# All of the second product in seven products, with casting loads and TensorE turns

## The chip, the cores and the metric

The kernel runs on one core of one Trainium2 chip. The metric is device time in microseconds (us), the median of several runs. One more execution was taken with the hardware profiler; durations in this text come from that one.

## The reference

Two stages. The first is linear attention with decay, for 4 batches, 8 heads, 768 positions and 64 features per head, computed in blocks of 64 positions with a running state; the second is a two-layer network with SiLU over the 3072 positions.

```python
for b in range(nb):                                  # 12 blocks of 64
    intra = np.einsum('bhic,bhjc->bhij', qb, kb) * Dmask[None]
    intra = np.einsum('bhij,bhjd->bhid', intra, vb)
    inter = np.einsum('bhid,bhde->bhie', qb * lam_pow[None], kv_state)
    out[:, :, sl] = intra + inter
    kb_dec = kb * rev_pow[None]
    kv_state = lam_block[None, :, None, None] * kv_state + np.einsum('bhsd,bhse->bhde', kb_dec, vb)
...
h = x @ w_in                       # 3072 x 512 by 512 x 2048
g = h * (1.0 / (1.0 + np.exp(-h)))
return (g @ w_out).astype(np.float32)   # 3072 x 2048 by 2048 x 512
```

All inputs and the output are 32-bit floats; the kernel's matmuls take bf16 and accumulate in 32 bits.

## The kernel before

**Units, sets, groups.** A unit is 128 positions of one batch, named (n, b): six values of n ("blocks 0 to 5" in the change's title) by four batches, 24 units. `rank` orders them: (0,0), (1,0), (0,1), (1,1) and so on for the first eight, then by n and batch. A set is two units whose k, q and v are loaded and prepared together: sets 0 to 3 pair n = 0 and 1 of a batch, sets 4 and 5 are n = 2, 6 and 7 are n = 3, 8 and 9 are n = 4, 10 and 11 are n = 5. A group is what the first product works on: four groups of two units (256 tokens), then four groups of four units (512 tokens).

**Loads.** SP's queue loads k, q and v of each set in 32 bits (`load_set`, lines 349 and 351), 0.5 MB each, into the buffers `ra` and `rb`. POOL's queue loads w_in and w_out in four slices each, cast to bf16 on the way (lines 364 and 367); a small `gate` copy (line 331) on POOL holds a slice back until k of a certain set has landed.

**Attention.** `prepare` casts k and q to bf16 (`kq`, on DVE or ACT), scales v (`vd`, on DVE or POOL) and turns k and q (`kqT`). Sets 0 to 3 are turned by TensorE (line 442: 8 transposes per burst, then two copies out of PSUM), sets 4 to 11 by a DMA transpose on SP's queue (line 622). Scores (`st_ps`), states (`d_ps`) and outputs (`x_ps`) are short bursts on TensorE (lines 463 to 543 and 647 to 687); masks, state updates (`yf`, `y`, `xf`, `xe`) and the evacuation to `xt` follow on DVE, ACT and POOL.

**First product.** `product1` (line 830) multiplies w_in by xt into a PSUM bank, and ACT writes SiLU of it to g (line 839). The last group goes through `product1_spared` (line 944): a two-by-two division of both factors with seven products in place of eight (Winograd's form), four rounds `jp`, with sums S1 to S4 of w_in and T1 to T4 of xt made by DVE. A round's seven products alternate between two PSUM banks P and R. After the first, P is copied to SBUF (`keep`), and further products accumulate on P; the products on R are completed by adding a kept copy (`total_of`, DVE).

**Second product.** The first eight units go through `product2_plain` (line 861): 16 matmuls of 512 columns per unit, one bank, one evacuation to `osb`, one store. The other 16 units go through `product2` and `products_of` (line 1072) in quads of four units, in the same seven-product form: sums `s` and, in place, `g` of the features (twelve on DVE, four on POOL per quad), sums `wsum` of w_out (`sums_of_w_out`; T1 overwrites a quarter of w_out, so it waits for all plain units), seven products of 16 matmuls of 256 columns, three copies of P (`keep`), three results that add a kept copy to R, and one plain copy of P. The last quad is divided into two parts that alternate.

**Order.** Nothing of this order is written by hand. Every piece is a `Task` with a priority key, the engines that it may run on with a cost for each, its dependencies and its buffers. `Planner.order` simulates the engines and three DMA queues and gives out tasks one by one; a task goes to the engine on which the plan ends it first. The program is then issued in that order; each engine works strictly in its order. Buffers come from small pools (`rb` 6, `kq` 3, `g` 18, `s` 12, `bank` 8 and others), and tasks that hold a counting buffer (`one`, `two`, `att`) limit how many banks each stage may hold.

Of the kernel before, what the change touches and what calls it, by code (L numbers as in the profile page):

```python
# [37 lines left out]
class Planner:  # L38

    LAT = {"PE": 0.23, "ACT": 0.06, "DVE": 0.06, "POOL": 0.08, "SP": 0.0}  # L40
    BEGIN = {"PE": 0.8, "ACT": 8.3, "DVE": 4.5, "POOL": 4.7, "SP": 0.8}
    FIRST, LAST, AHEAD = {"SP": 1.9, "ACT": 1.15, "POOL": 2.5}, 1.0, 0.75
# [13 lines left out]
    def order(self):  # L56
# [63 lines left out]
        while len(out) < len(self.tasks):  # L120
# [9 lines left out]
            for e in free:  # L130
# [8 lines left out]
                while ready[e]:  # L139
# [12 lines left out]
                    mine = now + t.on[e]  # L152
                    if any(max(free[o], now) + d < mine - 1e-9 for o, d in t.on.items() if o != e):
                        kept.append((key, i, t))
                        continue
# [33 lines left out]
def kernel(  # L189
# [27 lines left out]
    FRESH, TURNED, ALONE, LEAD = 4, 4, 6, 6.5  # L217
    SEQUENCE = "s0 i0 s1 i1 i2 s2 i3 o0 s3 o1 o2 o3 s4"
    POOLS = dict(bank=8, ra=3, rb=6, kq=3, kqT=3, vd=3, st=3, xe=6, xf=3, y=2, yf=2,
                 xt2=2, xt4=2, g=18, s=12, m=3, osb=3, one=3, two=4, att=6)  # L220
    BY_POOL, IN_BY_POOL, PLAIN, SPARED = (4,), (), 8, 1
# [116 lines left out]
    def load_set(key, si):  # L338
        n, b = sets[si][0]
        nb = 2  # L340
        rs = [Buf("ra" if si in (0, 3) else "rb") for _ in range(3)]
# [4 lines left out]
        def go(e, i):  # L346
            if n < PAIRED:
                tile_of(rs[i], [128, H, 2, 64], F32, "raw")
                nc.sync.dma_start(out=rs[i].tile.rearrange("p h e d -> p h (e d)"), in_=x[i])
            else:  # L350
                nc.sync.dma_start(out=tile_of(rs[i], [128, 2 * H, 64], F32, "raw"), in_=x[i])

        for i in range(3):
            ts.append([add((key, i), {"SP": 0.55}, lambda e, i=i: go(e, i), bufs=[rs[i]], nbytes=0.524,
# [55 lines left out]
    def key_of(si):  # L410
        u = rank[sets[si][0]]
        return u - 4.0 if sets[si][0][0] == 0 else u - LEAD
# [145 lines left out]
    def prepare(si):  # L558
# [7 lines left out]
        o.kq, o.kqT, o.vd, o.st = Buf("kq"), Buf("kqT"), Buf("vd"), Buf("st")  # L566
# [6 lines left out]
        def kq_of():  # L573
            return tile_of(o.kq, [128, nb, 2, NP, 2, 64], BF16, "kq")

        def kqT_of():
            return tile_of(o.kqT, [128, nb, 2, NP, U], BF16, "kqT")
# [9 lines left out]
        def cast(e, j, i):  # L587
            src = rs[i].tile[:, j * H:j * H + H, :].rearrange("p (m h) d -> p m h d", h=2)
            dst = kq_of()[:, j, i]
            copy(e, dst, src)  # L590

        ck = [[add((s - 1.0, i), {"DVE": 0.43, "ACT": 0.63}, lambda e, j=j, i=i: cast(e, j, i), deps=(lk, lq)[i],
                   bufs=[rs[i], o.kq]) for i in range(2)] for j in range(nb)]
        after("k", [t for ts in ck for t in ts])
# [10 lines left out]
        if si < TURNED:  # L605
            for j in range(nb):
                bank = Bank(fills=False)

                def turn(e, j=j, bank=bank):
                    t = tile_of(bank, [128, 2, NP, U], BF16, "tr")  # L610
                    for i in range(2):
                        for m in range(NP):
                            nc.tensor.transpose(t[:, i, m, :], kq_of()[:, j, i, m], ident)

                tr = add((s - 0.7, j), {"PE": 0.46}, turn, deps=ck[j], bufs=[bank, o.kq])
                for i in range(2):
                    o.turned.append(add((s - 1.0, 2), {"DVE": 0.43, "ACT": 0.6},
                                        lambda e, j=j, i=i, bank=bank: copy(e, kqT_of()[:, j, i], bank.tile[:, i]),
                                        deps=[tr], bufs=[bank, o.kqT]))
        else:  # L620
            def dma_turn(e):
                nc.sync.dma_start_transpose(kqT_of().rearrange("p b i m s -> p (b i m) s"),
                                            kq_of().rearrange("p b i m h d -> p (b i m h d)"))
# [4 lines left out]
    def first_part(o):  # L628
# [12 lines left out]
        def states(e):  # L641
            for j in range(nb):
                for m in range(NP):
                    for c in halves_of_d:
                        r = halves[c]
                        for p, rp in enumerate(halves):
                            nc.tensor.matmul(d_of(c)[rp, j, m, :], lhsT=o.kq_of()[r, j, 0, m, p, :],  # L647
# [3 lines left out]
        def scores(e):  # L651
            for j in range(nb):
                for m in range(NP):
                    for p, rp in enumerate(halves):
                        t = tile_of(st_ps[p], [128, nb, NP, 64], F32, "st_ps")
                        for c, r in enumerate(halves):
                            nc.tensor.matmul(t[r, j, m, :], lhsT=o.kqT_of()[rp, j, 0, m, r], rhs=o.kqT_of()[rp, j, 1, m, r],  # L657
# [6 lines left out]
    def second_part(o):  # L664
# [18 lines left out]
        def inter(e):  # L683
            for c in range(2):
                for j in range(nb):
                    for m in range(NP):
                        nc.tensor.matmul(x_of(c)[:, j, m, :], lhsT=o.xe[c].tile[:, (bs[0] + j) % 2, m, :],  # L687
                                         rhs=o.kqT_of()[:, j, 1, m, halves[c]],
# [196 lines left out]
    def sums_of_w_in():  # L885
# [6 lines left out]
        every = [t for o in infos for ts in o.ck for t in ts]  # L892

        def total(name, a, b, op, deps, on):
            done[name] = [add((on, 8), {"POOL": 2.4} if name in IN_BY_POOL else {"DVE": 0.70}, lambda e, ks=ks: tt(
# [3 lines left out]
        on = rank[groups[-SPARED][0]] - 4.0  # L899
# [6 lines left out]
    def product1_spared(gi, wbufs, wdone):  # L906
# [13 lines left out]
        done = {b: xt_done[gi] + xt_done[-1] for b in ("B11", "B21", "B22")}  # L920

        def total(name, a, b, op, deps, bufs):
            done[name] = [add((u0 - 2.0, 7), {"DVE": 0.42}, lambda e: tt(e, X(name), X(a), X(b), op), deps=deps, bufs=[x] + bufs)]
# [5 lines left out]
        for jp in range(4):  # L929
            P, R = Buf("bank"), Buf("bank")  # L930
            held = [P, R, Buf("att"), Buf("att")]
# [24 lines left out]
            wide, narrow = Buf("rb"), Buf("vd")  # L956

            def wide_of(wide=wide):
# [214 lines left out]
```

## Time and profile before

| | |
|---|---|
| median of 3 runs | 208.62 us (208.38 to 209.31) |
| the profiled execution, whole time | 207.82 us |
| its span, first to last instruction | 206.1 us |
| TensorE (PE) busy | 187.0 us, 91% |
| VectorE (DVE) busy | 134.8 us, 65% |
| ScalarE (ACT) busy | 107.4 us, 52% |
| GpSimd (POOL) busy | 52.4 us, 25% |
| mean granted TensorE clock | 0.989 |
| moved by DMA | 33.92 MB |

Shares are averages over the span; the page also cuts it into 40 slices of 5.15 us and gives each engine's busy share there in tenths. A group line names the source line, engine, operation, the tiles written and read, the shapes and the count; then busy time and the mean of one in ns; then the idle time before and who ended it. A line of the chain gives start, length and what ran. Many vector operations share line 320 (`tt`) and copies lines 313 (ACT) and 315 (DVE), so these are told apart by their tiles.

### The profile page before, as it was taken

The page shows a single profiled execution, that of the slowest core. Times are in us where ns is not written, and L with a number is a line of the kernel's source. Part 1 is how long each engine was busy: PE and PEld are TensorE (multiplying, and loading weights), DVE is VectorE, ACT ScalarE, POOL GpSimd, SP SyncE. Part 2 cuts the span into 40 slices and gives each one's busy share as a digit, 9 for nine tenths or more (in the row PEclk, how much of TensorE's full clock was granted, in tenths as well). Part 3 has the DMA queues.
Part 4 walks back from the last instruction along what each step waited for, and adds up shares of the span by engine and source line. Part 5 has one row for each costly group of instructions (what it writes and reads, how often), then busy time and mean ns, then how long its engine had stood idle before and what let it go on. Part 6 is the DMA issues. An engine that isn't in the chain of part 4 may idle for free.

```text
span 206.1 us, 5719 instructions
## 1 busy us (share of the span) xinstructions
PE 187.0 (91%) x2445; PEld 132.9 (64%) x2464; DVE 134.8 (65%) x249; ACT 107.4 (52%) x195; POOL 52.4 (25%) x76
## 2 busy tenths in 40 slices
PE   0459399999999999999999999998999999999993
PEld 0347288786667565544578648474675778888882
DVE  6488632767950467716989953999758995665411
ACT  3637267874336453375734492745615453766420
POOL 7231400401130111222565013346003221222200
PEclk9999889999999999999999999999999999999999
DMA  3999999999999999999999999905101110102213
GB/s 99 292 253 260 228 222 265 235 199 214 228 238 249 156 216 231 238 219 195 263 213 234 203 213 240 244 7 117 39 3 54 51 54 0 54 0 102 88 52 118
DMA packets 88617, 33.92 MB, mean 165 GB/s; under 512 B 67088, under 2 KB 87568, under 8 KB 88592
## 3 DMA queue, kind: packets, MB, share of 16 engines
q1 hardware_dynamic: 79232, 23.60, 57.3%
q0 software_dynamic: 4224, 4.19, 12.2%
q10 hardware_dynamic: 5136, 5.77, 8.7%
q8 instruction: 19, 0.31, 0.7%
q14 instruction: 6, 0.05, 0.1%
HBM read 27.27 MB, written 6.29 MB: 163 GB/s over the span
## 4 chain that ended last, share of the span: by engine, by line
PE 82%; DMA 8%; DVE 7%; issue 1%; ACT 0%; POOL 0%; POOLq 0%; DVEq 0%
PE h_ps L830 31%; PE o_ps L1072 22%; PE o_ps L861 13%; PE h_ps L944 6%; DMA w_in_bf<-in_moe_w_in_dram 5%; DMA raw<-in_k_dram 3%; PE x_ps L687 2%; DVE s L320 2%; PE tr L442 2%; DVE g L320 1%; PE d_ps L647 1%; PE x_ps L679 1%; PE st_ps L657 1%; PE x_ps L538 1%; DVE kq L315 1%
## 5 line engine op out<-in xcount | busy, mean ns | idle before, releaser
L830 PE MATMUL h_ps<-xt,w_in_bf 128*128 128x256 bf16 (+1 forms) x439 | 75.7, 322 | 4.7 <-DMA w_in_bf<-in_moe_w_in_dram 3.3
L839 ACT ACTIVATE g<-h_ps 128x512 bf16<-128x512 f32 x80 | 47.1, 594 | 45.7 <-PE h_ps L830 45.0
L830 PEld LDWEIGHTS <-w_in_bf 128*128 128x128 bf16 x448 | 43.7, 99 | 30.1 <-DMA w_in_bf<-in_moe_w_in_dram 3.5
L861 PE MATMUL o_ps<-w_out_bf,g 128*128 128x512 bf16 x118 | 29.7, 379 | 0.6 <-issue 0.2
L320 POOL TENSOR_TENSOR s<-g,s 128x512 bf16<-128x512 bf16 x16 | 19.0, 1188 | 43.1 <-DVE s L320 26.8
L320 DVE TENSOR_TENSOR st<-st_ps,tri 128x512 bf16<-128x512 f32 x32 | 20.5, 681 | 11.2 <-PE st_ps L657 11.2
L1072 PEld LDWEIGHTS <-g 128*128 128x128 bf16 x256 | 24.9, 98 | 4.4 <-ACT g L839 0.3
L320 DVE TENSOR_TENSOR xt<-x_ps,lam_xe 128x512 bf16<-128x512 f32 x24 | 15.9, 699 | 15.2 <-PE x_ps L687 9.5
L1072 PEld LDWEIGHTS <-s 128*128 128x128 bf16 x192 | 18.7, 98 | 2.6
L861 PEld LDWEIGHTS <-g 128*128 128x128 bf16 x128 | 12.1, 98 | 12.0
L320 POOL TENSOR_TENSOR vd<-raw,lam_v 128x512 bf16<-128x512 f32 x10 | 13.3, 1334 | 25.1 <-DMA raw<-in_v_dram 19.7
L313 ACT ACTIVATE kq<-raw 128x512 bf16<-128x512 f32 x27 | 16.2, 621 | 2.1 <-DMA raw<-in_q_dram 1.6
L320 DVE TENSOR_TENSOR osb<-o_ps,m 128x512 f32<-128x512 f32 (+1 forms) x15 | 8.7, 583 | 10.9 <-ACT m L313 6.8
L1072 PE MATMUL o_ps<-wsum,g 128*128 128x256 bf16 x128 | 15.3, 272 | 0.0
L1072 PE MATMUL o_ps<-w_out_bf,s 128*128 128x256 bf16 x128 | 15.3, 273 | 0.0
L442 PE MATMUL tr<-ident,kq 128*128 128x128 bf16 x64 | 7.0, 260 | 8.8 <-POOL gate L331 6.9
L1072 PE MATMUL o_ps<-w_out_bf,g 128*128 128x256 bf16 x128 | 15.0, 273 | 0.0
L320 DVE TENSOR_TENSOR s<-g 128x512 bf16<-128x512 bf16 x16 | 8.2, 510 | 10.4 <-ACT g L839 6.6
L313 ACT ACTIVATE m<-o_ps 128x512 f32<-128x512 f32 (+1 forms) x14 | 7.0, 503 | 11.4 <-PE o_ps L1072 11.4
L320 DVE TENSOR_TENSOR vd<-raw,lam_v 128x512 bf16<-128x512 f32 x14 | 9.2, 681 | 5.0 <-DMA raw<-in_v_dram 5.0
L313 ACT ACTIVATE osb<-o_ps 128x512 f32<-128x512 f32 (+1 forms) x12 | 6.7, 562 | 10.4 <-PE o_ps L861 6.5
L315 DVE CAST kq<-raw 128x512 bf16<-128x512 f32 x21 | 9.1, 451 | 3.8 <-DMA raw<-in_k_dram 2.0
(88 smaller groups left out, 215.1 us busy)
## 6 DMA issues: line engine op xcount, KB each, us to landing
raw<-in_k_dram SPq DMA_DIRECT2D x12, 512.0 KB, 8.2
raw<-in_q_dram SPq DMA_DIRECT2D x12, 512.0 KB, 8.5
raw<-in_v_dram SPq DMA_DIRECT2D x12, 512.0 KB, 8.0
out_dram<-osb ACTq DMA_DIRECT2D x20, 256.0 KB, 3.6
w_in_bf<-in_moe_w_in_dram POOLq DMA_DIRECT2D x4, 512.0 KB, 10.0
w_out_bf<-in_moe_w_out_dram POOLq DMA_DIRECT2D x4, 512.0 KB, 11.7
out_dram<-osb ACTq DMA_DIRECT2D x4, 128.0 KB, 1.7
out_dram<-osb SPq DMA_DIRECT2D x4, 128.0 KB, 1.7
```

Source lines behind the costliest of these rows:

```text
L313: nc.scalar.activation(o, i, AF.Copy)
L315: nc.vector.tensor_copy(o, i)
L320: (nc.vector if e == "DVE" else nc.gpsimd).tensor_tensor(o, a, b, op=op)
L442: nc.tensor.transpose(t[:, m, a], o.kq_of()[:, i, m, a], ident)
L538: nc.tensor.matmul(t[rh, m], lhsT=o.vd_of()[r, 2 * m + h, a, :], rhs=o.st_of(h)[r, m, a], start=m == 0 and a == 0, stop=True, skip_group_c ...
L647: nc.tensor.matmul(d_of(c)[rp, j, m, :], lhsT=o.kq_of()[r, j, 0, m, p, :], rhs=o.vd_of()[r, j, 2 * m + p, :], start=j == 0 and m == 0, sto ...
L687: nc.tensor.matmul(x_of(c)[:, j, m, :], lhsT=o.xe[c].tile[:, (bs[0] + j) % 2, m, :], rhs=o.kqT_of()[:, j, 1, m, halves[c]], start=False, s ...
L830: nc.tensor.matmul(t[:, j, :], lhsT=w_in_bf[:, ko, 128 * (m1 + j):128 * (m1 + j) + 128], rhs=xt[gi].tile[:, ko, :], start=(ko == 0), stop= ...
L839: nc.scalar.activation(t[:, half * per:half * per + per], bank.tile, AF.Silu)
L861: nc.tensor.matmul(t, lhsT=g.tile[:, j, 128 * gp:128 * gp + 128], rhs=w_out_bf[:, ko, :], start=(ko == 0), stop=(ko == KO - 1))
L944: nc.tensor.matmul(t[:, j, :], lhsT=W[w]()[:, k2, f:f + 128], rhs=X(r)[:, k2, :], start=first and j == 0 and k2 == 0, stop=True, skip_grou ...
L1072: nc.tensor.matmul(t[:, i_, :], lhsT=src(j)[:, k2, 128 * r:128 * r + 128], rhs=W[w]()[:, 2 * j + k2, :], start=first and i_ == 0 and j == ...
```

## The change

- `product2_plain` is used for no unit (`PLAIN` 8 to 0): the first eight units become two more quads of the seven-product form. T1 of w_out no longer waits for plain units. The first quad holds two of the four `two` buffers.
- `ONTO`: in the quads from rank 12 on, and in `product1_spared`, the first product on P is copied to the second bank R (by ACT or DVE), and the second product accumulates onto it; the result is then read from R alone. In `product1_spared` the SiLU of 1024 columns becomes two of 512, the first read straight from R.
- `CASTING`: k and q of sets 8 to 11 are loaded by DMAs on POOL's queue that cast to bf16, into one `rb` buffer laid out as `kq`; their casts go. The layout of `kq` and `kqT` of sets 4 to 11 puts k and q outermost.
- `TURNED` 4 to 6: sets 4 and 5 are turned by TensorE.
- In the planner, work on DVE is charged 0.2 us more when an engine is chosen (`BIAS`); costs of the sums are raised; the sums of w_in get a fixed priority (`SUMS_ON`) and wait for other tasks than before (`SUMS_AFTER`); the T sums of the last group no longer hold products back until the last xt.

```diff
+    BIAS = {"DVE": 0.2}
...
-                    mine = now + t.on[e]
-                    if any(max(free[o], now) + d < mine - 1e-9 for o, d in t.on.items() if o != e):
+                    mine = now + t.on[e] + self.BIAS.get(e, 0.0)
+                    if any(max(free[o], now) + d + self.BIAS.get(o, 0.0) < mine - 1e-9 for o, d in t.on.items() if o != e):
...
-    FRESH, TURNED, ALONE, LEAD = 4, 4, 6, 6.5
+    FRESH, TURNED, ALONE, LEAD = 4, 6, 6, 6.5
...
-                 xt2=2, xt4=2, g=18, s=12, m=3, osb=3, one=3, two=4, att=6)
-    BY_POOL, IN_BY_POOL, PLAIN, SPARED = (4,), (), 8, 1
+                 xt2=2, xt4=2, g=18, s=12, m=3, osb=3, one=3, two=4, att=6, sp=2)
+    BY_POOL, IN_BY_POOL, PLAIN, SPARED = (4,), (), 0, 1
+    CASTING, SUMS_AFTER, HURRY, SUMS_ON, HOLD, ONTO = 8, 16, 0.0, 9.0, 1, 12
...
+            elif si >= CASTING and i < 2:
+                tl = tile_of(rs[0], [128, 2, 2, NP, 2, 64], BF16, "kq")
+                nc.gpsimd.dma_start(out=tl[:, i].rearrange("p b m h d -> p (b m h) d"), in_=x[i])
...
+            if si >= CASTING and i < 2:
+                t = pool_task(add((key, i), {"POOL": 0.8}, lambda e, i=i: go(e, i), bufs=[rs[0]], nbytes=0.524, kind=CAST,
+                                  prior=pool_last[-1:] + raw[si - 1][1][2], late=2.0))
+                ts.append([t])
+                continue
...
-        o.kq, o.kqT, o.vd, o.st = Buf("kq"), Buf("kqT"), Buf("vd"), Buf("st")
+        o.kq, o.kqT, o.vd, o.st = rs[0] if si >= CASTING else Buf("kq"), Buf("kqT"), Buf("vd"), Buf("st")
...
-        every = [t for o in infos for ts in o.ck for t in ts]
+        every = [t for o in infos if rank[o.n, o.bs[0]] < SUMS_AFTER for t in o.cv] + [t for o in infos[:CASTING] for ts in o.ck for t in ts]
...
-        on = rank[groups[-SPARED][0]] - 4.0
+        on = SUMS_ON
...
-        done = {b: xt_done[gi] + xt_done[-1] for b in ("B11", "B21", "B22")}
+        done = {b: xt_done[gi] for b in ("B11", "B21", "B22")}
...
-            held = [P, R, Buf("att"), Buf("att")]
+            held = [P, R, Buf("sp")]
...
             m1 = product(0, P, "A11", "B11", True, [])
-            b1, c1 = keep("kqT", [m1])
-            m2 = product(1, R, "A12", "B21", True, [])
-            e11 = total_of(lambda w=wide_of: w()[:, :, lo], wide, b1, [m2, c1])
+
+            c1 = add((u0 - eager, 5), {"ACT": 0.6, "DVE": 0.69}, lambda e, P=P, R=R, f=bank_of: copy(e, f(R), f(P)), deps=[m1], bufs=[P, R])
+            m2 = product(1, R, "A12", "B21", False, [c1])
+            s11 = silu((low, lo), lambda R=R, f=bank_of: f(R), [m2], [R])
             m6 = product(2, P, "S2", "T2", False, [c1])
...
-            s1 = silu(lambda b=low: g_of(b), wide_of, 1.05, [e11, e12], [low, wide])
+            s12 = silu((low, hi), lambda h_of=h_of: h_of("12"), [e12], [narrow["12"]])
...
-        held = [P, R] + [Buf("two") for _ in range(2 * np_)]
+        held = [P, R] + [Buf("two") for _ in range(2 if u0 == PLAIN and HOLD else 2 * np_)]
...
         m1 = product(0, P, "A11", "B11", True, [])
-        b1, c1 = keep(0, [m1])
-        m2 = product(1, R, "A12", "B21", True, [])
-        e11 = result(0, lo, R, b1, [m2, c1])
+        if u0 >= ONTO:
+            c1 = add((s - eager, 5), {"ACT": 0.17 + 0.215 * np_, "DVE": 0.15 + 0.27 * np_},
+                     lambda e: copy(e, bank_of(R), bank_of(P)), deps=[m1], bufs=[P, R])
+            m2 = product(1, R, "A12", "B21", False, [c1])
+            e11 = result(0, lo, R, None, [m2])
+        else:
+            b1, c1 = keep(0, [m1])
+            m2 = product(1, R, "A12", "B21", True, [])
+            e11 = result(0, lo, R, b1, [m2, c1])
```

## The prediction

> **What bounds the kernel now.** I read the page's busy shares and slices first, then the busy time by stretches of 10 us, then the chain that ended last, then the groups by form. The page:
>
> ```profile
> PE 187.0 (91%) x2445; PEld 132.9 (64%) x2464; DVE 134.8 (65%) x249; ACT 107.4 (52%) x195; POOL 52.4 (25%) x76
> PE   0459399999999999999999999998999999999993
> DVE  6488632767950467716989953999758995665411
> DMA  3999999999999999999999999905101110102213
> ```
>
> The reader should see a PE row of nines from the eighth slice to the last but one, a DVE that is crowded only in places, and a DMA row that is full for the first 25 slices and then nearly empty. The table by stretches says how full the PE is (columns: window, its length, then PE, PEld, DVE, ACT, POOL busy, granted clock, DMA share, GB/s):
>
> ```profile
> 20.00:30.00 10.00, 6.66 (x132) 5.11 (x117) 5.43 (x11) 4.50 (x10) 2.41 (x5) 0.83 1.19 225
> 30.00:40.00 10.00, 9.95 (x148) 8.43 (x148) 4.18 (x9) 7.61 (x15) 2.41 (x4) 1.00 1.10 253
> 60.00:70.00 10.00, 9.89 (x125) 6.51 (x126) 0.87 (x2) 5.11 (x9) 1.04 (x1) 1.00 1.07 196
> 140.00:150.00 10.00, 9.32 (x58) 5.73 (x60) 8.26 (x14) 5.32 (x10) 3.15 (x3) 1.00 0.37 80
> 180.00:190.00 10.00, 10.00 (x94) 8.98 (x92) 6.20 (x12) 6.36 (x12) 2.29 (x2) 1.00 0.15 52
> ```
>
> From 30 to 200 us the PE is busy 168.2 of 170 us, at full granted clock. The only larger hole is one of 0.69 us at 140.6. So after about 24 us, when the second slice of w_in lands, time is the sum of PE work, plus 3.6 us of tail from 202.5 to 206.1. What the PE does in each piece, and its price, is in the chain (start, length, what):
>
> ```profile
> 13.71 10.23 DMA w_in_bf<-in_moe_w_in_dram
> 40.72 0.45 PE tr L442 x8
> 63.67 1.73 PE o_ps L861 x8
> 105.61 6.99 PE o_ps L1072 x64
> 140.58 0.05 issue
> 190.28 12.24 PE o_ps L1072 x112
> ```
>
> The profiled execution took 207.82 us for a span of 206.1; the median of the runs is 208.62. I work on the 207.82 and scale to the median at the end.
>
> **Products (removes PE work).** Eight 128-token units now use line 861: 16 matmuls of 512 columns each, 128 in all. The chain has 1.73 us per 8, so 27.7 us. Two quads of seven products replace them: 14 products of 16 matmuls of 256 columns, 224 in all. 6.99 us per 64 gives 24.5 us. Saving: 3.2 us, all on the PE and so on the path.
>
> **Turns of sets 4 and 5 (adds PE work).** Each set has two bursts of 8 transposes; 0.45 us per 8, four bursts, 1.8 us on the PE. Eight PSUM copies come with them (0.42 us on DVE or 0.60 on ACT, groups kqT<-tr), about 4 us, beside a DVE that has 0.87 us of work from 60 to 70 us. In return two DMA transposes leave SP's queue. Their issues hold SP 3.78 us (at 57.3) and 5.90 us (at 65.1), with the v load of set 5 queued behind the first and q, v of set 6 behind the second. Those loads move up by up to 9.7 us in all. This buys no PE time directly: it brings the first 512-token group, whose xt comes at 85 us now, nearer to 75.
>
> **Sums and evacuations (adds DVE, ACT, POOL work).** Each new quad needs 16 sums: 12 on DVE at 0.51, 0.42 and 0.61 us (rows s<-g, s<-s,g, g<-g), so 6.1 us, and 4 on POOL at 1.19, so 4.8 us. Two quads: 12.3 us of DVE, 9.5 us of POOL. They have 14 evacuations where there were 8, 6 more at 0.6 to 0.69, about 4 us. Hidden: DVE is free for 14 us between 50 and 80 (7.70, 0.87 and 7.10 busy), POOL for more. Without that cover up to 12 us would be late, and whoever reads the sums is the PE.
>
> **Casting DMAs (removes casts, moves issues).** Sixteen casts go (0.42 us on DVE, 0.62 on ACT): 6.7 to 9.9 us, off the path. Eight issues move from SP to POOL, whose queue also holds the xe blocks, the vd scalings and the fourth sums. Nearest row: the weight loads at line 364 and 367, 0.75 to 0.80 us an issue at 528 packets each. A k or q load has 2048 rows of 256 B, so between 0.75 us and four times that, 3.0 us: 6 to 24 us of POOL over some 50 us. I take 1 us each, nearest to the row; POOL is busy 25%. Each issue waits in POOL's order for a free buffer and for the previous set's v; behind it stand sums that a quad waits for. I cost it at 0, because between 100 and 160 us the PE always has a quad or a 512-token group in hand; without this cover, one late sum costs what the DVE chain at 129 to 140 us cost now, 0.69 us. Landing sooner is worth nothing either: the last loads go out at 127 and the PE has 42 us of work after the last xt at 160.6.
>
> A rule of the Trainium skill speaks against this edit. In the trace, POOL's vd at 55.87 took 2.81 us where its median is 1.04, while DVE ran wsum and kq casts beside it. The Trainium skill's page SBUF — State Buffer (Who interferes with whom) says that a DVE copy or cast in a 2-port mode locks GpSimd out, and that descriptors of a DMA issued from GpSimd are written through that port. By that rule each issue could wait behind such a cast. No row here shows a held issue.
>
> **First product copied to the second bank (moves a wait).** In the last three quads and in line 944's four rounds, the second product now waits for the copy of the first. One copy is 0.59 us (0.38 in the half-width parts). What was queued behind the first product on the PE is the second product; it can no longer follow at once. Cover: the chain alternates lines 944 and 1072 from 160 to 190, and the two halves of the last quad from 190.3 on, pieces of 0.44 to 1.75 us. I take 0; uncovered, 7 waits of 0.6 us, 4 us. In return four adds of 0.69 us leave DVE, and one SiLU of 1.05 becomes two of 0.6. DVE is not what PE waits for there (10.00 busy), so a gain of nothing. The planner's bias of 0.2 moves copies from DVE (65%) to ACT (52%); ACT takes 0.62 where DVE takes 0.42, so the startup chain, which has four kq casts and kqT copies, may lose or gain some 0.5 us. I take 0.
>
> **The early hole.** Plain units are the filler between 37 and 53 us, about 4.7 us of line 861. A quad cannot start there so freely: it needs both its groups' features, w_out's later slices (issued at 37.4 to 39.6, 11.7 us to landing), and sums made at 52.8 to 56.5. What can step in is line 830 of the third group (xt at 41.8 to 43.1): by 52.6, 160 of 192 available matmuls were done, so 32, or 3.5 us, and the first product, 1.75. But between 37.2 and 43.2 there are 1.77 us of plain work and only 0.87 us of line 830 to take its place. I charge 0.9 us, and set against it the 0.69 us hole at 140.6 and 0.2 us of small ones, since the supply comes earlier there.
>
> **Sum:** -3.2 + 1.8 + 0.9 - 0.9 = -1.4 us. 207.82 becomes 206.4; the median 208.62 becomes 207.2. About 0.5%, or 1.0 us, is what a measurement of this kernel can tell from no change.
>
> **Rivals.**
>
> *More than the sum: 205.6.* Loads that come ten us sooner, and a lighter DVE, close holes that I left open: the startup (gate copy at 13.59 behind an xe cast that waited 5.05 us for DVE, ahead of the 10.23 us weight load) up to 0.9, the middle 0.7. For it: the startup counts one to one. Against: the first loads and the gates are unedited.
>
> *Slower: quads 0 and 1 stand alone, 210.9.* Within a quad the first bank's fourth product follows its third with only a copy between: 0.6 us plus some 0.5 of hand-over. Line 830 fills such gaps in the quads of now. If nothing is there to fill them in the two new quads, the PE waits 1.1 us in each, and 0.6 more where the second quad's sums need s buffers of the first (12, all taken by one quad). The early hole stays and the holes at 140 are not closed: -1.4 + 0.9 + 2.2 + 0.6 = +2.3 us, 210.1 on the profiled run, 210.9 as a median. It decides if the PE's share from 40 to 75 us falls below nine tenths. For it: evacuations and sums take turns there with attention's own masks (DVE 8.12 from 40 to 50). Against: 11.3 us of line 830 (104 of the 256 matmuls of the first four groups) is still undone at 55 and can be mixed in, and DVE is idle from 60 to 70.
>
> *No change: POOL's queue gives it back, 208.6.* At 3.0 us an issue, eight issues add 24 us to a POOL that has 17.6 us of work from 90 to 140, and sums or xe blocks behind an issue come up to 3 us late. Two holes like the 0.69 us one at 140.6 would eat the 1.4. The rule on locked descriptors would work the same way. For it: the 2.81 row. Against: a quad's fourth sum is needed only by its last product.
>
> **Chances.** Forecast 0.50, more 0.15, slower 0.21, no change 0.14. The forecast's own range is 206.4 to 208.2, from the startup's 0.5 both ways and an uncovered wait or two; 0.43 of its 0.50 lies below 207.6, so faster by over 0.5% is 0.43 + 0.15 = 0.58. Within 0.5%: 0.07 of the forecast, 0.10 of the POOL case: 0.17. Slower: the rest, 0.25. The range that leaves out 2 in 10 goes from just under the gaining rival, 205.4, to the slow one, 210.9.
>
> **What would show it.** In the new profile line 861 is gone, line 1072 has 672 matmuls (448 now) at the same 1.75 per 16, and line 442 has 96. PE busy falls from 187.0 to about 185.6. A PE row with an eight or less between 40 and 75 us would show the slow rival; POOL issues over 2 us, with PE waits on s at 100 to 150, the POOL case. A first line 830 burst that starts other than at 24 us would show the startup moved. If PE busy itself is not 1.4 lower, the count is wrong. DMA should go slack before 125 us; if it does and the time does not move more, supply was not the bound.

## The result and the profile after

The changed kernel takes 210.09 us (median of 20 runs) beside 207.90 for the kernel before in runs on the same chips: 1.0102 times as long, 95% interval 1.0071 to 1.0132. The forecast was 207.2 against a median of 208.62, a gain of 0.7%. It came out 1.0% slower. Single executions of the kernel before spread from 206.05 to 209.31 and each profile is of one execution (for u_turn, u_onto and n_hold_s4a_on one of the longest, 224.17, 213.14 and 214.13 us), so below, ratios judge a kernel and profiles show where its time lies.

The changed kernel's profiled execution took 210.04 us with a span of 208.3. The page, its busy shares and rows:

```profile
PE 186.2 (89%) x2592; PEld 144.2 (69%) x2592; DVE 142.1 (68%) x252; ACT 111.6 (54%) x206; POOL 76.3 (37%) x100
PE   0459698989999997999997899999999999999993
DVE  6387822999999998946895983997653353555411
DMA  3999999999899999999999999800100210102203
```

PE busy fell, by 0.8 us (187.0 to 186.2). PE idle rose by 3.0 us (19.1 to 22.1), and the two together are the 2.2 us by which the span grew. DVE's row is a run of nines from the eighth slice to the fifteenth, where before it had digits down to 0. The table by stretches, same columns as before the change:

```profile
30.00:40.00 10.00, 9.27 (x144) 7.94 (x141) 5.01 (x10) 7.06 (x14) 2.68 (x5) 1.00 1.12 250
40.00:50.00 10.00, 9.21 (x198) 7.72 (x196) 9.83 (x19) 6.37 (x13) 3.25 (x6) 1.00 1.17 184
60.00:70.00 10.00, 10.00 (x199) 8.78 (x197) 10.00 (x16) 6.90 (x13) 3.91 (x5) 1.00 1.22 226
70.00:80.00 10.00, 8.21 (x170) 6.98 (x168) 9.94 (x17) 4.81 (x9) 6.19 (x7) 1.00 1.08 228
110.00:120.00 10.00, 7.79 (x158) 5.61 (x157) 7.84 (x11) 1.81 (x3) 8.76 (x9) 1.00 1.33 202
140.00:150.00 10.00, 10.00 (x161) 7.40 (x159) 7.30 (x13) 4.01 (x7) 3.10 (x3) 1.00 0.09 29
```

Two groups of holes are new: 3.8 us between 30 and 90 (0.6 before) and 2.2 us between 110 and 120 (0.2 from 90 to 120 before). After 120 us the PE has none; the hole at 140 is gone. Holes by stretch, PE idle in us, are the figure that the experiments use:

| | 30 to 90 | 90 to 120 | 120 to 150 |
|---|---|---|---|
| before | 0.6 | 0.2 | 0.85 |
| after | 3.8 | 2.2 | 0.0 |

The timeline of the PE names the longest of them; the brackets give the idle time ahead of the piece and what ended it:

```profile
42.32 2.78 PE L842 MATMUL h_ps<-xt,w_in_bf 128*128 128x256 bf16 x24 [0.79 <-DVE xt L322]
79.87 0.41 PE L699 MATMUL x_ps<-kqT,xe 128*128 128x64 bf16 x8 [1.37 <-POOL xe L319]
112.19 0.45 PE L669 MATMUL st_ps<-kqT 64*64 64x64 bf16 x32 [1.26 <-DMA kqT<-kq]
117.65 2.75 PE L842 MATMUL h_ps<-xt,w_in_bf 128*128 128x512 bf16 x12 [0.95 <-DVE xt L322]
```

and the chain that ended last shows how the third came about, a transpose that took 15.8 us from issue to landing:

```profile
94.79 1.53 PE o_ps L1086 x14
96.32 15.83 DMA kqT<-kq
...
112.38 1.05 POOL xf L322
...
113.46 1.36 DVE xe L317
```

The transposes by tile, first before, then after. Their number fell from 8 to 6, and the longest landing went from 8.7 to 15.8 us:

```profile
L622 SPq DMA_TRANSPOSE kqT<-kq x8: 1960/4807/5900, 57.3 to 140.3; - x8
DMA to landing us min/median/max: 4.5/6.8/8.7
```

```profile
L634 SPq DMA_TRANSPOSE kqT<-kq x6: 2796/4788/11888, 76.8 to 128.9; - x6
DMA to landing us min/median/max: 5.8/10.9/15.8
```

One stretch of DVE and of POOL, from the timelines of the changed kernel (its first row is DVE's, the others POOL's), shows what "full" means for DVE:

```profile
67.34 3.69 DVE L322 TENSOR_TENSOR s<-g 128x512 bf16<-128x512 bf16 x2
```

```profile
66.96 1.04 POOL L322 TENSOR_TENSOR xf<-y,lam_be 128x512 f32<-128x512 f32 x1 [0.27 <-PE h_ps L842]
68.07 0.68 POOL L319 CAST xe<-xf 64x512 bf16<-64x512 f32 x1
68.72 2.03 POOL L322 TENSOR_TENSOR vd<-raw,lam_v 128x512 bf16<-128x512 f32 x2
76.71 1.22 POOL L355 DMA_DIRECT2D kq<-in_k_dram  x1
77.92 1.16 POOL L355 DMA_DIRECT2D kq<-in_q_dram  x1
79.12 0.69 POOL L319 CAST xe<-yf 64x512 bf16<-64x512 f32 x1
```

Two sums that take 0.41 us each when undisturbed took 3.69 together, and ended 0.3 us after POOL's run of work. The whole trace shows the same. By tile, with the shortest, median and longest duration in ns:

```profile
L322 DVE TENSOR_TENSOR s<-g x24: 411/425/2830, 40.1 to 194.1; 128x512 bf16<-128x512 bf16 x24
L322 DVE TENSOR_TENSOR st<-st_ps,tri x32: 673/681/692, 13.3 to 149.0; 128x512 bf16<-128x512 f32 x32
```

Of the 24 sums s<-g, which read SBUF alone, 17 ran with POOL idle, or all but idle, and took 0.41 to 0.43 us; the seven that ran beside POOL's work took 1.28 us in the mean. DVE's casts of k and q (kq) go from 0.42 to as much as 1.37 us in the same way. The masks st, which read a PSUM bank, took 0.67 to 0.69 us, although 18 of the 32 ran beside POOL's work. If the time of every DVE operation above the shortest of its kind and shape is added up, an estimate from the trace, it is 20.5 us here and 11.1 us before.

The last three of POOL's rows above are the 1.37 us hole at 79.87: the xe cast that the PE needs stands behind two casting issues in POOL's order.

### The profile page after: what moved, and what is told of

Same layout as the page of the kernel before. It is cut to its first block, busy times and chain, and to the rows that moved or that the text cites. A ratio compares the mean times of both kernels' runs of the same rounds, so it can differ in the third digit from the quotient of the medians.

```text
span 208.3 us, 6044 instructions
## 1 busy us (share of the span) xinstructions
PE 186.2 (89%) x2592; PEld 144.2 (69%) x2592; DVE 142.1 (68%) x252; ACT 111.6 (54%) x206; POOL 76.3 (37%) x100
## 3 DMA queue, kind: packets, MB, share of 16 engines
q0 software_dynamic: 20736, 6.29, 30.5%
## 4 chain that ended last, share of the span: by engine, by line
PE 52%; DMA 18%; DVE 16%; SPq 7%; issue 2%; POOL 2%; ACT 1%; DVEq 0%; POOLq 0%; ACTq 0%
PE o_ps L1086 24%; PE h_ps L842 18%; DMA raw<-in_v_dram 9%; DMA kqT<-kq 8%; SPq L352 7%; PE h_ps L956 6%; DVE s L322 4%; DVE st L322 2%; DVE xt L322 2%; DVE wsum L322 2%; DVE g L322 1%; PE x_ps L699 1%; DVE vd L322 1%; DVE kq L317 1%; POOL kq L355 1%
## 5 line engine op out<-in xcount | busy, mean ns | idle before, releaser
L322 POOL TENSOR_TENSOR s<-g,s 128x512 bf16<-128x512 bf16 x24 | 28.3, 1180 | 56.9 <-DVE s L322 42.4
L1086 PEld LDWEIGHTS <-s 128*128 128x128 bf16 x288 | 27.9, 98 | 4.5 <-issue 0.4
L322 DVE TENSOR_TENSOR s<-g 128x512 bf16<-128x512 bf16 x24 | 15.9, 673 | 13.4 <-ACT g L851 11.2
L1086 PE MATMUL o_ps<-w_out_bf,s 128*128 128x256 bf16 x192 | 22.9, 273 | 0.4 <-DVE osb L322 0.4
L1086 PE MATMUL o_ps<-w_out_bf,g 128*128 128x256 bf16 x192 | 22.8, 273 | 0.4 <-DMA w_out_bf<-in_moe_w_out_dram 0.4
L1086 PE MATMUL o_ps<-wsum,g 128*128 128x256 bf16 x192 | 22.8, 273 | 0.0
L315 ACT ACTIVATE m<-o_ps 128x512 f32<-128x512 f32 (+1 forms) x16 | 8.7, 543 | 13.9 <-PE o_ps L1086 13.3
L315 ACT ACTIVATE kq<-raw 128x512 bf16<-128x512 f32 x24 | 14.0, 619 | 0.5 <-ACT osb L315 0.5
L322 DVE TENSOR_TENSOR g<-g 128x512 bf16<-128x512 bf16 x24 | 12.5, 520 | 0.0
L322 DVE TENSOR_TENSOR s<-s,g 128x512 bf16<-128x512 bf16 x24 | 11.7, 490 | 0.6
L1086 PE MATMUL o_ps<-wsum,s 128*128 128x256 bf16 x96 | 11.5, 273 | 0.0
## 6 DMA issues: line engine op xcount, KB each, us to landing
w_out_bf<-in_moe_w_out_dram POOLq DMA_DIRECT2D x4, 512.0 KB, 11.7
kq<-in_q_dram POOLq DMA_DIRECT2D x4, 256.0 KB, 12.5
```

What stands on the lines that cost most here:

```text
L315: nc.scalar.activation(o, i, AF.Copy)
L322: (nc.vector if e == "DVE" else nc.gpsimd).tensor_tensor(o, a, b, op=op)
L1086: nc.tensor.matmul(t[:, i_, :], lhsT=src(j)[:, k2, 128 * r:128 * r + 128], rhs=W[w]()[:, 2 * j + k2, :], start=first and i_ == 0 and j == ...
```

## The experiments

Four theories were tried against each other. *D*: the PE waits between 30 and 90 us because the two new quads overfill DVE. *L*: DVE is overfilled by length, not by count: its work is stretched while POOL runs. *T*: casting loads in POOL's queue make a DMA transpose land late, which is the hole after 110. *S*: without the TensorE turns the supply of 512-token work comes too late. The expectations of the first runs call D by the letter P, and T, in a wider form, by C; E and Q are explained in the expectations that test them. Every edit is planned anew, so the order of work differs a little everywhere; that limits each reading. Ratios are to the kernel before.

**Undoing one part.** Each starts from the changed kernel.

```diff
u_plain:  PLAIN 0 -> 8       u_cast:  CASTING 8 -> 99
u_turn:   TURNED 6 -> 4      u_onto:  ONTO 12 -> 99, and product1_spared as before
```

> The changed kernel with the first eight units back on single products (PLAIN 8); casting loads, turns and the copy to the second bank stay. Theory P (the two new quads overfill DVE and POOL between 40 and 90 us, and the PE waits for it): the PE holes between 30 and 80 us shrink from 3.8 us to about 1 and DVE's share from 40 to 90 falls from 9.8 of 10 to about 7.5; PE work grows by 3.2 us; time about 209, close to the changed kernel or 1 us less. Theory C (casting loads on POOL delay the transposes and the sums): the 2.2 us hole at 110 to 120 stays and the time is 212 or more.

> The changed kernel with k and q of sets 8 to 11 loaded by SP in 32 bits and cast on DVE or ACT as before (CASTING 99). Theory C: the hole of 2.2 us between 110 and 120 us closes, POOL is some 9.5 us less busy, the time falls to about 208. Theory P: the holes from 30 to 80 us stay at about 3.8 us, casts come back on a full DVE and ACT, the time stays at 210 or rises.

> The changed kernel with sets 4 and 5 turned by DMA transposes again (TURNED 4). By the count alone the PE loses 1.8 us of work and the time falls to about 208.3. Theory P: eight copies fewer on a full DVE, so at least that. Theory S (supply: without the turns the first 512-token group comes late and the two new quads stand alone): PE holes between 60 and 90 us grow by 2 us or more and the time is 210 or above.

> The changed kernel with the first partial product kept in SBUF again, in the quads and in the last group (no copy to the second bank). If the wait of the second product for the copy is covered, PE is 10.00 of 10 from 160 to 190 as before and the time stays at 210. If not, it falls by up to 4 us. Theories P and C expect no change beyond 0.5 us.

| | us | ratio, 95% | holes 30 to 90 | 90 to 120 | 120 to 150 |
|---|---|---|---|---|---|
| u_plain | 210.4 | 1.0153 (1.0118 to 1.0188) | 1.0 | 2.75 | 0.3 |
| u_cast | 211.18 | 1.0185 (1.0141 to 1.0230) | 4.2 | 0.2 | 2.6 |
| u_turn | 218.14 | 1.0496 (1.0456 to 1.0536) | 3.6 | 2.45 | 8.5 |
| u_onto | 212.19 | 1.0199 (1.0149 to 1.0248) | 3.3 | 2.7 | 0.2 |

No part alone is the culprit; without any of them the rest is as slow or slower. But the holes sort themselves: those of 30 to 90 shrink to 1.0 us without the new quads and stay without the casting loads, the one of 90 to 120 shrinks to 0.2 without the casting loads and stays without the quads. Without casting loads a third group opens at 120 to 150, where DVE is busy for 27.2 of 30 us instead of 22.4; that the casts which came back are its cause is likely and not shown.

Without the turns the time rises by 8 us, where the count says 1.8 less. Part of S is in the trace: the first 512-token group starts at 91.0 us instead of 81.9, and products of the quads wait 2.0 us for evacuations (`m`, `osb`) from 70 to 90 us instead of 0.4. But PE idle from 60 to 90 did not grow by 2 us as S expected (2.0 us, 1.8 in the changed kernel). The extra idle time lies at 120 to 150, and 7.37 us of it are one gap at 123.67, in the middle of a burst, for which the profile names no releaser; the granted clock of that stretch is 0.83. So the price of the missing turns is measured and most of its cause is open.

The run u_onto expected no change and came out 2 us slower than the changed kernel, but its trace does not place them at the copy that it takes out. From 160 to 190 us, where most of the copies stand, the PE is busy for 29.89 of 30 us without them and 30.00 with them; in the changed kernel's trace the first copy comes at 142 us, and the longest hole of u_onto is earlier:

```profile
114.61 0.64 PE L669 MATMUL st_ps<-kqT 64*64 64x64 bf16 x32 [2.25 <-DMA kqT<-kq]
```

It is the wait for set 8's transpose again, which took 18.8 us in this order of work, and the granted clock from 110 to 120 us is 0.83 (1.00 in the changed kernel).

**The new quads alone, on the kernel before.** `PLAIN` 8 to 0 on the kernel before, nothing else.

> The kernel of before with only PLAIN set to 0: two more quads of seven products, everything else as it was. The count says 3.2 us less PE work. Theory S (late supply): sets 4 and 5 still come by DMA transposes, so the first 512-token group comes at 85 us or later and the two quads, with DVE's sums, have to fill 55 to 85 alone: PE holes of 5 us or more between 30 and 150, time 210 to 214. If the turns were needless, 206 to 208.

212.2 us, 1.0232 (1.0184 to 1.0280). PE idle is 4.2 us from 30 to 90 and 3.7 from 120 to 150. By itself the largest saving of the count, 3.2 us, is a loss of 2.3%. Sets 4 and 5 are not turned by TensorE here, the first 512-token group starts at 91.1 us, and products of the quads wait 2.9 us for evacuations from 70 to 90 us: the prediction's slower rival, in a kernel without the turns.

**The quads without their feature sums.**

```diff
+        if u0 >= 8:
             for j in range(4):
                 ...                      # the four sums
+        if u0 < 8:
+            A.update(S1=natural("A21"), S2=natural("A11"), S3=natural("A21"), S4=natural("A12"))
```

> The changed kernel, with the feature sums of the two new quads (units 0 to 7) left out: their products read unsummed features in place of S1 to S4, so the output of the first 1024 tokens is another; the PE's matmuls, the sums of w_out and the evacuations stay as they are. Theory D (in 30 to 90 us the PE waits for DVE, which those sums fill): DVE falls from 54.2 to about 42 us busy of the 60, the PE's holes there from 3.8 us to about 1, and the time to about 207.3. Theory E (the early holes come from data: w_out's slices and v of sets 2 and 3 land too late for quads that need whole groups): the holes stay above 3 us and the time at about 210.

207.53 us, 1.0020 (0.9987 to 1.0053): 0.8% below the changed kernel. The windows of this run:

```profile
30.00:60.00 30.00, 29.34 (x451) 25.63 (x450) 20.97 (x38) 20.01 (x37) 6.00 (x10) 1.00 1.19 228
60.00:90.00 30.00, 29.89 (x442) 22.39 (x445) 20.77 (x35) 15.78 (x27) 13.54 (x13) 1.00 1.26 204
90.00:120.00 30.00, 27.55 (x459) 19.91 (x462) 26.34 (x43) 11.95 (x20) 17.47 (x17) 1.00 1.51 183
```

DVE is busy for 41.7 us of the 60 instead of 54.2 and the PE's holes fall from 3.8 to 0.8. So data (w_out, v of sets 2 and 3) was there in time, but for less than a microsecond; the sums are what the PE waited for (D, not E). The holes at 90 to 120 stay in size, 2.45 us, though not in kind: the longest, 1.50 us, ends with DVE's xt and none with a transpose.

**Fourth sums on DVE instead of POOL.** `BY_POOL` empty, with casting loads (c_s4dve) and without, with `SUMS_ON` 16 (n_s4cast, to be read beside n_cast16).

> The changed kernel with the fourth feature sum of all quads on DVE instead of POOL: POOL loses 28 us of work, DVE gets 24 sums of 0.42 us more, 10 us. Theory L (DVE's work is stretched by POOL's: a sum of 0.41 us takes up to 2.8 us beside POOL's): DVE's busy time rises by clearly less than 10 us or falls, the longest s<-g drops below 1.5 us, the time falls by 1 us or more. Theory D without L (DVE is simply too full): DVE's busy time rises by 10 us, holes between 30 and 90 us grow, and the time rises by 1 to 3 us.

> The changed kernel without casting loads (CASTING 99) and with the sums of w_in at their old, late priority (SUMS_ON 16). If the casting loads alone opened the hole at 110 to 120 us, and the early sums of w_in the one at 120 to 150 that came without them, both close: 2.2 and 2.6 us, the time is about 208.5 to 209, and the holes at 30 to 90 (about 4 us) are what is left above the count. If the w_in sums are not the cause of the second hole, it stays at 2.6 us and the time at 211.

> The changed kernel without casting loads and with the late sums of w_in (as the run n_cast16, 209.5 us), and with the fourth feature sum on DVE. No casting load blurs the picture here. Theory L (POOL's work stretches DVE's): DVE's busy time stays within 3 us of n_cast16's 146.7 although 24 sums of 0.42 us, 10 us, are added, and the holes at 30 to 90 and 120 to 150 us (3.1 and 2.3 us) shrink; time 207 to 209. Theory D without L: DVE at about 157 us, holes larger, time 211 or more.

| | us | ratio, 95% | DVE busy | holes 30 to 90 | 90 to 120 | 120 to 150 |
|---|---|---|---|---|---|---|
| c_s4dve | 214.17 | 1.0334 (1.0279 to 1.0389) | 139.5 | 2.7 | 7.0 | 0.2 |
| n_cast16 | 209.54 | 1.0089 (1.0059 to 1.0118) | 146.7 | 3.1 | 0.2 | 2.3 |
| n_s4cast | 209.32 | 1.0057 (1.0035 to 1.0079) | 142.7 | 2.1 | 1.1 | 1.0 |

In both pairs DVE got 24 sums more, 10 us by their length, and its busy time fell: by 2.6 us with casting loads, by 4.0 without. That is L. The time did not follow: with casting loads the holes at 90 to 120 grew to 7 us, of which 5.86 are one wait for set 8's transpose (19.6 us to landing); without them the two intervals overlap. My expectation of 1 us or more for c_s4dve was a miss: DVE's length is not alone in setting the PE's waits. n_cast16 also answers its own question with no: late sums of w_in do not close the hole at 120 to 150.

**Keeping casting loads away from transposes.** n_cast10 casts only sets 10 and 11; n_hold leaves all casting loads but orders them:

```diff
     for si in range(len(sets)):
         prepare(si)
+    for si in range(CASTING + 2, len(sets)):
+        raw[si][1][0][0].deps += infos[si - 2].turned
```

> The changed kernel with casting loads for sets 10 and 11 only. Theory T (a DMA transpose that is issued while four casting loads are in POOL's queue takes 15.8 us to land instead of 7): set 8's transpose meets no casting load, lands in 9 us or less, and the 1.26 us hole at its scores goes; casts of sets 8 and 9 come back on DVE and ACT. Time 208.5 to 210. If the hole at 90 to 120 us stays above 1.5 us, the transposes were not its cause.

> The changed kernel with one more dependency: the casting loads of sets 10 and 11 are issued only after the transposes of sets 8 and 9 have landed. Nothing else is edited. Theory T: set 8's transpose shares the DMA engines with two casting loads instead of four, lands in 11 us or less, the hole at 90 to 120 us shrinks from 2.2 to under 1 us and the time to about 208.5 to 209, unless the later loads open a hole of their own after 120 us.

n_cast10: 210.05 us, 1.0090 (1.0052 to 1.0128); holes at 90 to 120 fall to 0.8, but 1.2 come at 120 to 150 and 3.3 stay at 30 to 90. Set 8's transpose took 11.8 us and not the expected 9 or less: two casting loads of set 10 were in flight when it was issued. n_hold: 207.74 us, 0.9983 (0.9954 to 1.0011), 1.2% below the changed kernel by one dependency (and the new order that comes with it). Its windows and its transposes:

```profile
60.00:90.00 30.00, 28.15 (x432) 22.05 (x431) 29.38 (x46) 17.66 (x32) 17.75 (x17) 1.00 1.22 195
90.00:120.00 30.00, 29.79 (x467) 20.81 (x469) 24.91 (x40) 13.96 (x24) 18.66 (x19) 1.00 1.50 174
120.00:150.00 30.00, 29.89 (x389) 20.04 (x389) 17.74 (x29) 14.87 (x25) 11.30 (x11) 1.00 0.69 98
```

```profile
L634 SPq DMA_TRANSPOSE kqT<-kq x6: 1432/4098/9123, 76.2 to 127.4; - x6
DMA to landing us min/median/max: 5.8/8.0/13.9
```

The holes after 90 us are 0.3 us together; the median landing fell from 10.9 to 8.0. Set 8's transpose is the longest of the six in both kernels. It took 13.9 us where 11 or less was expected, but it was also issued 2.4 us earlier, so it landed at 107.8 us instead of 112.1, and no product waited for it.

The kept traces say how a transpose depends on the casting loads. Set 8's took 4.9 to 8.8 us where no casting load was in flight at its issue (six runs, u_cast with 7.2 among them), 9.1 to 16.2 with two (seven runs) and 15.6 to 19.6 with three or four (five runs; a sixth, u_turn, has 11.7). In the changed kernel, from 80 to 110 us, the DMA share was 1.50 to 1.78 at 156 to 196 GB/s, where it was 1.03 to 1.24 at 216 to 239 GB/s before. T holds as far as these runs go: the holes at 90 to 120 are 0.2 us without casting loads (u_cast, n_cast16; the 1.1 of n_s4cast end mostly with ACT's g) and in n_hold, and 2.2 to 7.0 us in four kernels that issue them unheld and wait for this transpose (the changed kernel, u_plain, u_onto, c_s4dve). A late transpose is not always a hole, though: in x_nosums it took 15.6 us and nothing waited. Nor does holding two loads back always do: in n_hold_s4a_on's profile the transpose took 16.2 us with two in flight, and the PE waited 2.55 us. The 3.3 us at 30 to 90 are untouched.

**What is left.** Four runs add one thing each to n_hold: the fourth sums of the two new quads on DVE (n_hold_s4a), the dependency for sets 8 and 9 as well (n_hold8), both (n_hold8_s4a), no feature sums in the two new quads (x_hold_nosums).

```diff
-    ... {"POOL": 1.25} if x in BY_POOL else ...
+    ... {"POOL": 1.25} if x in BY_POOL and u0 >= 8 else ...      # n_hold_s4a, n_hold8_s4a
-    for si in range(CASTING + 2, len(sets)):
+    for si in range(CASTING, len(sets)):                          # n_hold8, n_hold8_s4a
```

> The run n_hold and, besides, the fourth feature sums of the two new quads on DVE (the other quads keep them on POOL). Theory L: DVE's busy time from 30 to 90 us stays at 54 us or falls although 8 sums, 3.4 us, are added, the holes there fall from 3.8 to 2.7 us as they did with all fourth sums moved, and the time is 1 us below n_hold's, 207.5 to 208.

> The run n_hold with its dependency on sets 8 and 9 too: no casting load is issued before the transposes of the sets two ahead of it (6 and 7 for 8 and 9) have landed. Theory Q (POOL's order: the two casting issues at 76.2 and 77.4 us, 1.2 us each, stand ahead of the xe cast that the PE waits 1.37 us for at 79.3): that hole goes, the holes at 60 to 90 us fall from 1.85 to about 0.5, the time to 206 to 206.5, unless set 8 then comes late and a hole after 100 us takes its place. If the hole at 79 stays, the xe cast is late for another reason.

> The run n_hold8 with the fourth sums of the two new quads on DVE. In n_hold this took DVE's busy time from 30 to 90 us from 54.7 to 48.9 us and the holes there from 3.3 to 2.6, but opened 1.8 us at 90 to 120. With both edits theory L and theory Q add up: holes at 30 to 90 of 1.5 us or less, time 205.5 to 207.

> The run n_hold, with the feature sums of the two new quads left out (the output of the first 1024 tokens is another). If the transposes and these sums are the two whole causes and add up, both groups of holes close, 30 to 200 us has less than 1.5 us of PE idle, and the time is 205 to 205.5: the count of PE work with the startup's 1 us on top. If it stays above 206.5, a third cause is missing.

| | us | ratio, 95% | DVE 30 to 90 | holes 30 to 90 | 90 to 120 | 120 to 150 |
|---|---|---|---|---|---|---|
| n_hold | 207.74 | 0.9983 (0.9954 to 1.0011) | 54.7 | 3.3 | 0.2 | 0.1 |
| n_hold_s4a | 209.01 | 1.0024 (0.9993 to 1.0054) | 48.9 | 2.6 | 1.8 | 0.2 |
| n_hold8 | 211.79 | no interval | 52.8 | 4.1 | 0.0 | 0.7 |
| n_hold8_s4a | 208.0 | 1.0013 (0.9989 to 1.0036) | 49.5 | 2.1 | 0.9 | 0.7 |
| x_hold_nosums | 207.88 | 1.0001 (0.9975 to 1.0028) | 41.9 | 1.4 | 1.8 | 0.7 |

None of the four came out at its expected time. n_hold_s4a is the cleanest reading of L: eight sums more on DVE (3.4 us) and 5.8 us less busy time, so eight sums of 1.18 us on POOL had cost DVE some 9 us, if nothing else differs between the two orders. The sum of DVE's time above the shortest of each kind, the estimate used above, falls from 22.1 to 8.1 us over the span, which agrees. The runs of n_hold8 spread from 208.4 to 213.2 us, too far for an interval. It took the casting issues away from the xe cast, and the 1.37 us hole at 79 did go from its timeline; a 1.31 us one in front of xt at 83.06 came in its place (Q half right, no gain). The same wait of 1.31 us for xt stands at 81 to 83 us in u_cast, n_cast16 and n_cast10, where no casting issue is that early, so in these orders nothing was gained by clearing the way for the xe cast. x_hold_nosums is the miss that matters: the two causes do not add up. Its early holes are 1.4 us, but 1.8 open at 90 to 120, where DVE is busy 26.95 of 30 us with sums of w_in and evacuations, and the time is that of n_hold. A sum of causes, each shown alone, is not the time of their joint removal.

**The planner's surcharge and the place of the w_in sums.** `BIAS` 0.2 to 0.0 on n_hold (n_hold_bias0); `SUMS_ON` 9 to 14 on n_hold and n_hold_s4a.

> The run n_hold with the planner's DVE surcharge back at 0. If the surcharge helps by keeping copies off the full DVE between 30 and 90 us, the holes there grow past 3.3 us and the time rises to 208.5 or more; if it only shifts work, the time stays within 0.5 us of 207.7.

> The run n_hold_s4a with the sums of w_in at a later priority (SUMS_ON 14 instead of 9), so that they leave DVE between 86 and 115 us to the attention's work. In n_hold_s4a PE waited 0.77 us at 110 for xt, behind DVE's sums. Theory D/L: the holes at 90 to 120 us fall from 1.8 to under 0.7, those at 30 to 90 stay at 2.6, and the time is 206 to 207.2, below the kernel of before (207.9). If the holes only move past 120 us, it stays at 208 to 209.

> The run n_hold with SUMS_ON 14 alone. Its holes after 90 us are already 0.3 us, so no gain is to be had: 207.5 to 208. If it gets slower, the early sums of w_in were of use in themselves.

n_hold_bias0: 215.9 us, 1.0372 (1.0326 to 1.0418). I had priced the surcharge at 0 with 0.5 either way; it is worth 3.9% here, against n_hold: without it the holes from 30 to 90 grow to 5.4 us and DVE from 90 to 120 to 29.47 of 30. n_hold_s4a_on: 208.82, 1.0033 (0.9998 to 1.0068); n_hold_on: 208.1, 1.0008 (0.9977 to 1.0039). Neither gains, against an expected 206 to 207.2 for the first. No version tried beats the kernel before; n_hold cannot be told from it.

## Why the prediction was wrong, step by step

*What bounds the kernel: right as far as it went.* PE work plus holes is the time; both were read correctly for before.

*The count: right, by the prices of its pieces.* 16 matmuls of line 1086 take 1.75 us as those of line 1072 did, and 16 transposes of sets 4 and 5 take 0.89 us (four bursts, 1.8 us). The prediction's own sign for a wrong count was a fall of PE busy other than 1.4 us, and it fell by 0.8; but busy time does not tell the count that finely. The trace before lacks 19 of 2464 matmul records, which shows as gaps of 0.05 us that count as idle there and shortens its busy time by about 1 us. The other way, it holds a stretch that the prediction passed over, though it showed the row with 0.83 for 20 to 30 us: from 24.2 to 27.6 us the granted clock was 0.50, after 3.3 us without PE work.

```profile
23.99 3.41 PE h_ps L830 x16
28.87 1.75 PE h_ps L830 x16
```

The same 16 matmuls took 3.41 us there and 1.75 us afterwards, so that execution carries about 1.7 us that the profile of the changed kernel does not have.

*"The early hole", +0.9: the first step that failed.* 3.8 us were measured from 30 to 90 against 0.6 before, so 3.2 us more where the sum has 0.9. I counted which matmuls were available and not who had to make their operands. The cover was named, "DVE is free for 14 us between 50 and 80", and was wrong twice. It was summed over 30 us, while the sums are due from 40 us on, among attention's masks. And the sums were priced at mean durations of a stage in which POOL is quieter. DVE's busy time from 30 to 90 rose by 19.5 us (34.7 to 54.2); x_nosums gives back 12.5 of it and 3.0 us of hole.

*"Casting DMAs: I cost it at 0": the second step that failed.* The issue price was right, 1.16 to 1.22 us against the 1 taken. What was not priced is the other queue: SP's transposes land later while casting loads are in flight, and the one of set 8, issued after four of them at 88 to 92 us, took 15.8 us (7.2 in u_cast). The term, taken as 0, was 2.0 us of hole (2.2 against 0.2). The two failed terms together are 4.3 us above the sum (2.3 and 2.0); the span missed it by 3.6, with 1.0 us more of PE busy time in the first 30 us going the other way. I had moved the casts' DMAs past POOL's order but not past SP's. The argument that the PE "always has a quad or a group in hand" failed with it: the scores of set 8 stand in the PE's order ahead of that other work, so one late transpose held the PE up for 1.26 us there and, by way of xf, xe and xt, for 0.95 us at 117.65.

*The credits, 0.9: earned.* The hole at 140 closed (0.85 us of idle from 120 to 150 before, none after).

*First product copied to the second bank, 0: not contradicted.* With the copies the PE is busy for 30.00 of 30 us from 160 to 190, so they were covered; the 2 us of u_onto stand elsewhere, as said above. *The surcharge, 0 with 0.5 either way:* on n_hold it is worth 8 us (n_hold_bias0), more than any term of the sum. *Turns:* the price was right, the use was not. The first 512-token group starts at 81.9 us (85.1 before) and not near 75, and "this buys no PE time directly" holds for the count, but u_turn is 8 us slower.

*The rivals.* The slower one, 210.9, was close to 210.09, and its sign came, an eight in the PE row at 41.7 to 46.9 us. That is luck more than insight: of the waits inside the two quads, 0.42 us at 74.13 is the only one of its kind in the timeline, and the hole of that slice is a wait for xt. Its mechanism shows only where the turns are missing (b_plain0, u_turn). The POOL rival had the right suspect for the wrong reason: no casting issue was held, none took over 1.22 us. The gaining rival's startup came in part: PE busy in the first 30 us was 1.0 us more (16.3 to 17.3), and more than that in work, as the clock was 0.50 for 3.4 us before; over the later runs the figure goes from 15.9 to 18.5, so much of it is scatter.

*The rule of the Trainium skill.* The Trainium skill's page SBUF — State Buffer (Who interferes with whom) says that a DVE copy or cast in a 2-port mode can lock GpSimd out of descriptor writing. Here all eight issues took 1.16 to 1.22 us, the one at 114.48 beside a DVE cast (xe) for 0.34 us of it, so no run shows it. The same section of the Trainium skill says that a DVE instruction with two SBUF inputs contends with a GpSimd instruction that reads SBUF. The trace agrees: s<-g takes 0.41 us alone and up to 2.83 us beside POOL's xe and vd; DVE's casts, with one input, were stretched too (kq to 1.37 us). I cited the half that spoke of the DMA and passed over the half that bears on the sums.

*What stays open.* Why holes return elsewhere when a cause is removed, and why the turns are worth 8 us. Each edit gives a new order on every engine, and no run here separates "DVE is full wherever sums are put" from "the planner, which knows nothing of the DVE and POOL clash, places them badly". That the transposes are slowed in the DMA engines themselves is argued from the DMA share and the landings; no view gives the engine of a packet.

## What to carry to other kernels

When an in-order engine runs at nine tenths, count who must finish before each piece of work can start, in the very ten microseconds in which it is due; spare time elsewhere in the span is no cover. A DMA that is moved to another queue can still delay the queue it left: ask which transfer there is late next. And when an edit moves the order of everything, a part undone alone says which hole belongs to it, not what its removal is worth; and before a part is given a price, see whether the hole of the run stands where the part does (u_onto's did not).

## What the hardware showed that I had not expected

Work on POOL cost DVE more here than it saved: eight sums of 1.18 us on POOL kept DVE busy some 9 us longer, against 3.4 us for doing them on DVE itself (n_hold against n_hold_s4a, as far as the two orders are otherwise alike). A casting load of 2064 packets (20,736 of the software queue less the 4,224 of the weights, by 8) took POOL 1.16 to 1.22 us to issue, against 0.75 us for a weight load of 528 (0.96 for the first of the eight), so the price grew far less than the packets. Set 8's DMA transpose took 15.6 to 19.6 us from issue to landing with three or four casting loads in flight in five of six runs, and 4.9 to 8.8 with none. And stretches of 3.4 us at half the granted clock followed gaps in the PE's work: 3.3 us without work in the kernel before (clock 0.50 from 24.2 to 27.6 us), a gap of 2.25 us in u_onto (0.51 from 114.6 to 118.0); the gaps of the changed kernel after 20 us, 1.90 us at most, were followed by none.
